# The second matrix product of seven token blocks as seven block products (Strassen's scheme, Winograd's form), with its operand sums on VectorE

## The chip, the core and the metric

One NeuronCore of a Trainium2 chip. TensorE (PE) multiplies matrices into PSUM, VectorE (DVE) and ScalarE (ACT) work elementwise between SBUF and PSUM, GpSimd (POOL) and SyncE (SP) here mostly issue transfers. The metric is the device time of one execution in microseconds; lower is better.

## What is computed

Linear attention with a cosine weight, then a feed-forward layer with a sigmoid GELU. q, k, v have 8 batches, 8 heads, 576 tokens and 64 features; the layer has d_model 512 and d_ff 2048.

```python
def phi(x, c, s):
    r = np.maximum(x, 0.0)
    return np.concatenate([r * c, r * s], axis=-1)     # c, s: cos, sin of pi/2 * pos / S
q_p, k_p = phi(q, cos_w, sin_w), phi(k, cos_w, sin_w)
kv  = np.einsum('bhsf,bhsd->bhfd', k_p, v)
z   = np.sum(k_p, axis=2)
num = np.einsum('bhsf,bhfd->bhsd', q_p, kv)
den = np.einsum('bhsf,bhf->bhs', q_p, z)[..., None] + 1e-06
x   = (num / den) as (B * S, 512)
h   = x @ w_in                                          # 512 -> 2048: the first product
g   = h * (1.0 / (1.0 + np.exp(-1.702 * h)))
out = g @ w_out                                         # 2048 -> 512: the second product
```

## The kernel before

The order of all work is written out by hand: each engine runs its instructions in the order in which the program names them, and semaphores hold an instruction until its operands are there and its target is free. A transfer belongs to the queue of the engine that issues it, so on SP and POOL a transfer that waits also holds those behind it.

**Blocks.** Of each batch 512 tokens form one block; the last 64 tokens of every batch, the tails, are gathered in `xt` and go through both products together at the end. Batch 0 is laid out in its own way and runs first (L474 to L614, together with the beginning of block 1 in `start_block`, L452). The loop at L643 then makes blocks 1 to 7. While block b is in its two products, everything for the attention of batch b + 1 is made beside it.

**One pass of the loop, in program order:**
- First product (`mm1`, L391): 16 chunks `fc` of 128 of the 2048 hidden features, each four matmuls of 512 columns (L383, the tokens are the columns) into a PSUM bank, then the GELU on ScalarE (`gelu`, L386), which writes the chunk as bf16, 128 features by 512 tokens, into a buffer `g` of its own. Block 1 has its first five chunks in `start_block`.
- Ahead of its first chunk: the weighted relu of q for batch b + 1 (`trig_q`, L189, ten instructions on VectorE), each of five chunks followed by a transposing transfer on SP into `qT` (`qturn_dma`, L223).
- Ahead of its second chunk: the same for k, and the copy of v to bf16 (`kv_operands`, L624), then `load_q` for batch b + 2 on SP.
- Between the products: `kv_next` (L616), the product of k and v for batch b + 1 into a buffer of `pat` (PSUM, two buffers), and its evacuation `kvs` by VectorE. In block 1 it stands behind the first token tile of the second product.
- Second product (`mm2`, L427): four tiles `t` of 128 tokens. A tile is 16 matmuls (L432): the weights loaded into the array are 128 features by 128 tokens of `g`, the columns that stream are 512 columns of `w_out_sb`. ScalarE evacuates a tile to `ysb` (L436), POOL sends it out (L439). Token 4p + t of a block is row p of tile t.
- Between half tiles: `x_next` (L637) for the five token tiles of batch b + 1. Each is a numerator on TensorE (`num_mm`, L328, into `pat`), three instructions on VectorE (`num_div`: L339, L341, L343, giving `xn`) and a transposing transfer on SP into `xT` (`xturn_dma`, L372). Behind `x_next(3)` stands `load_kv` (L146) for batch b + 2 on SP.
- In block 7 there is no next batch. The tails go through the first product (`mm1_tails`) and the second (tile 4 of `mm2`) ahead of its own second product, whose last tile is made as two halves of 256 columns so that the last transfer is short.

**Layouts of k and v.** Batches 1 and 2 have k and v in `kf`, `vf` with nine tokens a partition and two heads on the two halves of the partitions (`load`, L124; `trig`, L165; `vcopy`, L191; `kv_mm`, L236: 72 matmuls with 64 rows each). Batches 3 to 7 have four tokens a partition and all 128 partitions (`load_chunks`, L127; `trig_q` with `kr2`; `kv_chunks`, L244: 40 matmuls of 65 columns).

**Buffers.** `pmm` has four PSUM banks, used in turn by both products; `gpool` has 20 buffers `g` of 128 by 512; `ypool` four buffers `ysb`.

Of the kernel before, what the change touches and what calls it, by code (L numbers as in the profile page):

```python
# [14 lines left out]
MAX = mybir.AluOpType.max  # L15
PSUM = bass.MemoryType.PSUM
# [3 lines left out]
def kernel(  # L20
# [9 lines left out]
    nc = tc.nc  # L30
# [12 lines left out]
    gpool = ctx.enter_context(tc.tile_pool(name="gpool", bufs=20))  # L43
# [17 lines left out]
    kf, vf = [t[:, 0:NI * S].rearrange("p (i e) -> p i e", i=NI) for t in (kf2, vf2)]  # L61
    vb = raw("vb", BF16)
# [44 lines left out]
    kr = one.tile([128, NS, NI, 128], BF16, name="kr")  # L107
    vt = one.tile([128, NS, NI, VW], BF16, name="vt")
# [8 lines left out]
    nc.gpsimd.memset(vt[:, :, :, 64:66], 1.0)  # L117
# [5 lines left out]

    def load(t, src, b, eng=nc.gpsimd):  # L124
        eng.dma_start(out=t, in_=src_of(src, b))
# [20 lines left out]
    def load_kv(b):  # L146
        if b < 3:
            load(kf, k, b, nc.sync)
            load(vf, v, b, nc.sync)
        else:  # L150
            load_chunks(kf2, k, b, nc.sync)
            load_chunks(vf2, v, b, nc.sync)
# [38 lines left out]
    def vcopy(i0, i1, act=False):  # L191
        o = vt[:, :, i0:i1, 0:64].rearrange("p j i e -> p i j e")
        i = vf[:, i0:i1].rearrange("p i (j e) -> p i j e", e=64)
        if act:
            nc.scalar.activation(o, i, AF.Copy)
        else:
            nc.vector.tensor_copy(o, i)
# [188 lines left out]
    def gelu(fc):  # L386
        g = gpool.tile([128, MT], BF16, name="g")
        nc.scalar.activation(g, hp.pop(fc), AF.Gelu_apprx_sigmoid)  # L388
        gT[fc] = g
# [37 lines left out]
    def mm2(b, t, lo, hi, c0=0, c1=d_model, end=False):  # L427
        if lo == 0:
            yp[b, t, c0] = pmm.tile([128, d_model], F32, name="mm")
        for fc in range(lo, hi):  # L430
            w = gT[fc][:, ts(t, 128)] if t < 4 else gt[:, fc, ts(b // 2, 128)]
            nc.tensor.matmul(yp[b, t, c0][:, c0:c1], w, w_out_sb[:, fc, c0:c1],  # L432
                             start=(fc == 0), stop=(fc == FC - 1))
        if hi == FC:
            ysb = ypool.tile([128, d_model], F32, name="ysb")
            nc.scalar.activation(ysb[:, c0:c1], yp[b, t, c0][:, c0:c1], AF.Identity)  # L436
            for p0, n, dst in rows(b, t):
                eng = nc.sync if end else nc.gpsimd
                eng.dma_start(out=dst[:, c0:c1], in_=ysb[p0:p0 + n, c0:c1])  # L439

    def idle(n, cols=512):
        w = pmm.tile([128, 512], F32, name="mm")
        for _ in range(n):
            nc.tensor.matmul(w[:, 0:cols], warm[:, 0:128], warm[:, 0:cols], start=True, stop=True)
# [3 lines left out]

    def vt_rhs(r, i, j):
        return vt[r, j, i, 0:65]  # L450
# [48 lines left out]
    load(kf, k, 1)  # L499
# [72 lines left out]
    load(vf, v, 1)  # L572
# [4 lines left out]
    for j in range(NS):  # L577
        trig(kr, kf, j)
# [7 lines left out]
    vcopy(0, 2)  # L586
    vcopy(2, 4, act=True)
# [7 lines left out]
    kv_open()  # L595
    kv_mm(0, 4, vt_rhs, 0, 65)
    kv_evac(0, 4)
# [18 lines left out]
    def kv_next(b):  # L616
        if b < 3:
            kv_open()
            kv_mm(0, 4, vt_rhs, 0, 65)
            kv_evac(0, 4)  # L620
        else:
            kv_chunks()

    def kv_operands(b):  # L624
        if b < 3:
            for j in range(NS):
                trig(kr, kf, j)
            vcopy(0, 4)
        else:
            for c in range(5):  # L630
                trig_q(c, dst=kr2, src=kf2)
            for c0, c1, n in ((0, 4, 128), (4, 5, 64)):
                i = vf2[:, 0:2048] if c0 == 0 else vf2[0:64, 2048:2560]
                nc.vector.tensor_copy(vt2[0:n, c0:c1, :, 0:64],  # L634
                                      i.rearrange("p (h c d) -> p c h d", h=H, c=c1 - c0))
# [5 lines left out]


    for b in range(1, B):  # L643
        nb = b + 1 if b + 1 < B else None
        f0 = 5 if b == 1 else 0
        for fc in range(f0, FC):
# [4 lines left out]
            if nb is not None and fc == f0 + 1:  # L651
                kv_operands(nb)

                if nb + 1 < B:
                    load_q(nb + 1, nc.sync)
            mm1(b, fc)
        if nb is not None:
            x_open(nb)
        if nb is not None and b > 1:
            kv_next(nb)  # L660
        if nb is None:
            for fc in range(FC):
                mm1_tails(fc)
            for u in range(1, B, 2):
                mm2(u, 4, 0, FC, end=(u > 3))
        for t in range(4):
            if nb is None:
                for c in range(2 if t == 3 else 1):
                    n = 256 if t == 3 else 512
                    mm2(b, t, 0, FC, c * n, c * n + n, end=True)  # L670
                continue
            for u in range(2):
                mm2(b, t, 8 * u, 8 * u + 8)
                s = 2 * t + u
                if s == 1 and b == 1:

                    kv_next(nb)
                c = s if b > 1 else s - 1
                if b == 1 and s == 2:
                    x_next(nb, 0)  # L680
                if 0 <= c < 5 and (b > 1 or c > 0):
                    x_next(nb, c)
                if c == 3 and nb + 1 < B:
                    load_kv(nb + 1)
# [30 lines left out]
```

## Time and profile before

| what | value |
| --- | --- |
| runs | 291.19, 291.25, 291.77 us, median 291.25 |
| span of the profiled execution, first to last instruction | 289.4 us |
| granted TensorE clock | 1.000 |
| VectorE busy, block from 142.2 to 172.3 | 15.55 us, 38 instructions |
| ScalarE busy, same block | 11.94 us, 20 instructions |
| mean DMA share, same block | 0.87 |
| DMA share 172 to 180, 180 to 187, 187 to 195, 195 to 202 | 1.14, 0.94, 0.72, 0.67 |
| transposing transfers into qT: number, median from issue to landing | 35, 3.5 us |
| transposing transfers into xT: the same | 24, 2.7 us |
| k of batches 3 to 7, issue to landing | 6.9 us |
| v of batches 3 to 7, issue to landing | 11.0 us |

The page gives the profiled execution's span; a time of its own beside that is not among the runs. Times in the views are microseconds from the start of the span. The duration of a VectorE instruction overlaps the beginning of the next: the relus of 128x512 last 0.48 us and start 0.395 us apart. A line of the chain of waits in order of time has start, duration, engine, buffer, line and number of instructions; a line of the groups has the busy time, the mean of one in ns, and the idle time ahead of them with what ended most of it; a line of the timeline has start, duration, engine, line, operation, and in brackets how long the engine had been idle and what it waited for. The DMA share is the busy share of 16 engines summed over queues, so that it can come out over 1.

### The profile page before, as it was taken

What the parts mean: (1) busy time and instruction counts of PE and PEld (TensorE: products, weight loads), DVE (VectorE), ACT (ScalarE), POOL (GpSimd) and SP (SyncE); (2) the same over time, 40 slices, a digit from 0 to 9 for tenths busy, and PEclk for the clock granted to TensorE, in tenths of its full rate; (3) what the DMA queues carried; (4) which work ended last, traced back from release to release, by engine and by line L of the source; (5) the groups of instructions that cost most, each with busy time, mean ns of one, the idle gap of its engine ahead of it and who ended that gap; (6) DMA issues with size and microseconds to landing.
All of it is one profiled execution on the core that took longest, in us unless ns stands there. A gap on an engine that the chain in (4) does not pass through costs nothing.

```text
span 289.4 us, 5412 instructions
## 1 busy us (share of the span) xinstructions
PE 282.1 (97%) x2140; PEld 154.9 (54%) x2172; DVE 121.9 (42%) x323; ACT 128.0 (44%) x223; POOL 37.1 (13%) x69
## 2 busy tenths in 40 slices
PE   8999999999999999999999999999999999999995
PEld 2675646755555554555455545554555455554444
DVE  4834435772657266624670567148614300000000
ACT  6966644662146314631364126511760157761111
POOL 6683004100110011001100110001000100002000
PEclk9999999999999999999999999999999999999999
DMA  7999999999699899996999589967992610002322
GB/s 242 242 214 292 284 236 202 354 309 223 162 226 241 200 219 251 230 219 158 228 286 215 127 228 257 203 177 200 290 157 61 113 55 1 2 0 45 86 89 73
DMA packets 83545, 53.51 MB, mean 185 GB/s; under 512 B 57888, under 2 KB 78112, under 8 KB 83520
## 3 DMA queue, kind: packets, MB, share of 16 engines
q1 hardware_dynamic: 77456, 36.97, 57.2%
q0 software_dynamic: 6064, 16.19, 20.6%
q8 instruction: 17, 0.28, 0.4%
q14 instruction: 8, 0.07, 0.1%
HBM read 36.70 MB, written 9.44 MB: 159 GB/s over the span
## 4 chain that ended last, share of the span: by engine, by line
PE 92%; DMA 3%; ACT 2%; DVE 1%; issue 1%; ACTq 0%; POOL 0%
PE mm L432 42%; PE mm L383 37%; PE mm L411 4%; PE at L328 3%; DMA vb<-in_v_dram 2%; PE at L249 2%; PE at L241 1%; ACT g L388 1%; DMA kf<-in_k_dram 1%; PE at L360 1%; PE mm L404 1%; DVE xn L343 0%; PE mm L209 0%; ACT xT L367 0%; DVE xh L309 0%
## 5 line engine op out<-in xcount | busy, mean ns | idle before, releaser
L432 PE MATMUL mm<-w_out_sb,g 128*128 128x512 bf16 (+1 forms) x508 | 116.1, 372 | 1.2 <-issue 0.2
L383 PE MATMUL mm<-xT,w_in 128*128 128x512 bf16 (+1 forms) x582 | 112.1, 348 | 0.5
L388 ACT ACTIVATE g<-mm 128x512 bf16<-128x512 f32 x128 | 75.6, 598 | 32.5 <-PE mm L383 32.4
L383 PEld LDWEIGHTS <-w_in 128*128 128x128 bf16 x592 | 60.6, 113 | 48.7
L432 PEld LDWEIGHTS <-g 128*128 128x128 bf16 x528 | 48.8, 98 | 49.6
L436 ACT ACTIVATE ysb<-mm 128x512 f32<-128x512 f32 (+1 forms) x37 | 21.7, 586 | 111.2 <-PE mm L432 111.2
L439 POOL DMA_DIRECT2D out_dram<-ysb x36 | 19.7, 548 | 221.3 <-ACT ysb L436 221.3
L343 DVE TENSOR_TENSOR xn<-at,inv 128x512 bf16<-128x512 f32 x39 | 27.0, 691 | 1.3
L339 DVE TENSOR_SCALAR den<-at 128x8 f32<-128x8 f32 x36 | 6.0, 166 | 29.8 <-PE at L328 29.7
L328 PEld LDWEIGHTS <-qT 128*128 128x128 bf16 x312 | 14.4, 98 | 7.5
L189 DVE TENSOR_SCALAR qn<-qf,cosw 128x512 bf16<-128x512 f32 (+1 forms) x33 | 15.8, 478 | 3.9 <-DMA qf<-in_q_dram 3.9
L189 DVE TENSOR_SCALAR kr<-kf,cosw 128x512 bf16<-128x512 f32 (+1 forms) x25 | 12.0, 480 | 11.9 <-DMA kf<-in_k_dram 11.9
L328 PE MATMUL at<-kvs,qT 128*128 128x65 bf16 x312 | 15.8, 193 | 0.0
L189 DVE TENSOR_SCALAR qn<-qf,sinw 128x512 bf16<-128x512 f32 (+1 forms) x33 | 15.8, 478 | 0.0
L252 DVE CAST kvs<-at 128x520 bf16<-128x520 f32 x5 | 3.5, 702 | 27.3 <-PE at L249 27.3
L432 PE MATMUL mm<-w_out_sb,gt 128*128 128x512 bf16 x62 | 13.9, 379 | 0.1
L411 PE MATMUL mm<-xt,w_in 128*128 128x448 bf16 x64 | 12.3, 352 | 0.0
L173 DVE TENSOR_SCALAR kr<-kf,cosw 128x256 bf16<-128x256 f32 x24 | 9.0, 376 | 7.4 <-DMA kf<-in_k_dram 7.4
L189 DVE TENSOR_SCALAR kr<-kf,sinw 128x512 bf16<-128x512 f32 (+1 forms) x25 | 12.0, 479 | 0.0
L634 DVE CAST vt<-vf 128x2048 bf16<-128x2048 f32 (+1 forms) x10 | 7.9, 820 | 6.6 <-DMA vf<-in_v_dram 6.6
L432 PEld LDWEIGHTS <-gt 128*128 128x128 bf16 x64 | 6.3, 98 | 7.5
L413 ACT ACTIVATE gt<-mm 128x448 bf16<-128x448 f32 x16 | 8.7, 543 | 3.3 <-PE mm L411 3.2
(93 smaller groups left out, 129.3 us busy)
## 6 DMA issues: line engine op xcount, KB each, us to landing
qf<-in_q_dram SPq DMA_DIRECT2D x6, 1024.0 KB, 6.3
out_dram<-ysb POOLq DMA_DIRECT2D x24, 256.0 KB, 4.0
kf<-in_k_dram SPq DMA_DIRECT2D x5, 1024.0 KB, 6.9
vf<-in_v_dram SPq DMA_DIRECT2D x5, 1024.0 KB, 11.0
w_out_sb<-in_moe_w_out_dram POOLq DMA_DIRECT2D x4, 512.0 KB, 17.7
out_dram<-ysb POOLq DMA_DIRECT2D x12, 128.0 KB, 6.3
kf<-in_k_dram POOLq DMA_DIRECT2D x1, 1152.0 KB, 13.4
vf<-in_v_dram POOLq DMA_DIRECT2D x1, 1152.0 KB, 21.0
```

The source lines that it names most:

```text
L173: eng.tensor_scalar(o, i, 0.0, w[:, j:j + 1], op0=MAX, op1=MUL)
L189: nc.vector.tensor_scalar(o, i, 0.0, sc, op0=MAX, op1=MUL)
L328: nc.tensor.matmul(ps[:, h // 4, ds((h % 4) * 65, 65)], qT[:, h, ts(c, 128)], kvs_of(h), start=not eps_too, stop=(not eps_too or h % 4 == ...
L343: nc.vector.tensor_tensor(xn, pv[:, :, :, 0:64], inv.unsqueeze(3).to_broadcast([128, 2, 4, 64]), op=MUL)
L383: nc.tensor.matmul(hp[fc][:, t0:t1], wcol(kc, fc), x[b][:, kc, t0:t1], start=(kc == 0), stop=(kc == KC - 1))
L388: nc.scalar.activation(g, hp.pop(fc), AF.Gelu_apprx_sigmoid)
L411: nc.tensor.matmul(hps[:, 64:B * 64], wcol(kc, fc), xt[:, kc, 64:B * 64], start=(kc == 0), stop=(kc == KC - 1))
L413: nc.scalar.activation(gt[:, fc, 64:B * 64], hps[:, 64:B * 64], AF.Gelu_apprx_sigmoid)
L432: nc.tensor.matmul(yp[b, t, c0][:, c0:c1], w, w_out_sb[:, fc, c0:c1], start=(fc == 0), stop=(fc == FC - 1))
L436: nc.scalar.activation(ysb[:, c0:c1], yp[b, t, c0][:, c0:c1], AF.Identity)
L439: eng.dma_start(out=dst[:, c0:c1], in_=ysb[p0:p0 + n, c0:c1])
L634: nc.vector.tensor_copy(vt2[0:n, c0:c1, :, 0:64], i.rearrange("p (h c d) -> p c h d", h=H, c=c1 - c0))
```

## The change

**The second product of blocks 1 to 7.** The block's activations are split in two token halves i and two feature halves j (A_ij: 256 tokens by 1024 features), `w_out` in two feature halves and two column halves (W_jk: 1024 by 256). Eight block products would give the four output blocks; the changed kernel makes seven:

| product | into bank | activations | weights |
| --- | --- | --- | --- |
| p1 | x | A00 | W00 |
| p2 | w | A01 | W10 |
| p6 | x, added to p1 | s2 = s1 - A00 | t2 = W11 - t1 |
| p5 | y | s1 = A10 + A11 | t1 = W01 - W00 |
| p7 | x, added | s3 = A00 - A10 | t3 = W11 - W01 |
| p3 | y, added to p5 | s4 = A01 - s2 | W11 |
| p4 | x, added | A11 | nt4 = W10 - t2 |

The outputs are out00 = p1 + p2, out11 = (p1 + p6 + p7) + p5, out01 = (p1 + p6) + (p5 + p3), out10 = p1 + p6 + p7 + p4. A product is two tiles of 128 tokens with eight matmuls of 256 columns each, 112 matmuls in all. A bank holds both tiles (two times 256 columns). ScalarE keeps copies of x after p1 and after p6 and of y after p5 (`keep`, in buffers `kept_*`), VectorE adds a bank and a copy into `ysb` (`join`, after p2, p7 and p3), ScalarE evacuates x after p4. Each output leaves as one transfer with pieces of 256 columns.

**Sums on VectorE.** The weight sums t1, t2, t3, nt4 are made once (`w_sums`, four instructions of 128x2048 bf16), ahead of the loop, into `wsum`. The activation sums are made in each block in two halves of four chunks (`g_sums`, eight instructions of 128x1024 bf16) into `sums`: s3 and the first half of s1, s2, s4 at chunk 12 of the first product, the second half of s1 and s2 after `x_next(0)`, that of s4 after p1. `g` becomes a buffer of four chunks (five buffers), so that a sum is one instruction.

**Places of other work.** In blocks 2 to 6 the k-v product stands ahead of chunk 14 of the first product, and `x_next(0)` ahead of p1; `x_next(1)` to `(4)` follow p1, p2, p6, p5. In block 1 the k-v product follows p2, `x_next(0)` and `(1)` follow p6, the others p5, p7, p3.

**k and v of batches 1 and 2** use the layout of batches 3 to 7; `kr` and `vt` go, batch 0's `kr` lies in `wsum`, its `vb` in `sums`.

```diff
-    gpool = ctx.enter_context(tc.tile_pool(name="gpool", bufs=20))
+    gpool = ctx.enter_context(tc.tile_pool(name="gpool", bufs=5))
...
-    vb = raw("vb", BF16)
+    sums = one.tile([128, 4, d_ff], BF16, name="sums")
+    vb = sums.rearrange("p n e -> p (n e)")[:, 0:NI * S].rearrange("p (i e) -> p i e", i=NI)
...
+    wsum = one.tile([128, 4, d_ff], BF16, name="wsum")
+    kr = wsum.rearrange("p n e -> p (n e)")[:, 0:NS * NI * 128].rearrange(
+        "p (j i f) -> p j i f", j=NS, i=NI)
...
     def load_kv(b):
-        if b < 3:
-            load(kf, k, b, nc.sync)
-            load(vf, v, b, nc.sync)
-        else:
-            load_chunks(kf2, k, b, nc.sync)
-            load_chunks(vf2, v, b, nc.sync)
+        load_chunks(kf2, k, b, nc.sync)
+        load_chunks(vf2, v, b, nc.sync)
...
     def gelu(fc):
-        g = gpool.tile([128, MT], BF16, name="g")
-        nc.scalar.activation(g, hp.pop(fc), AF.Gelu_apprx_sigmoid)
-        gT[fc] = g
+        if fc % 4 == 0:
+            gT[fc // 4] = gpool.tile([128, 4, MT], BF16, name="g")
+        nc.scalar.activation(gT[fc // 4][:, fc % 4], hp.pop(fc), AF.Gelu_apprx_sigmoid)
...
+    def w_sums():
+        tt = nc.vector.tensor_tensor
+        tt(wt["t1"], wq[0, 1], wq[0, 0], op=SUB)
+        tt(wt["t2"], wq[1, 1], wt["t1"], op=SUB)
+        tt(wt["t3"], wq[1, 1], wq[0, 1], op=SUB)
+        tt(wt["nt4"], wq[1, 0], wt["t2"], op=SUB)
...
+    def g_sums(names, h):
+
+        tt = nc.vector.tensor_tensor
+        o = {n: sg[n][:, ts(h, 4)] for n in sg}
+        for n in names:
+            if n == "s1":
+                tt(o[n], a_blk(1, h), a_blk(1, h + 2), op=ADD)
+            elif n == "s2":
+                tt(o[n], o["s1"], a_blk(0, h), op=SUB)
+            elif n == "s3":
+                tt(o[n], a_blk(0, h), a_blk(1, h), op=SUB)
+            else:
+                tt(o[n], a_blk(0, h + 2), o["s2"], op=SUB)
...
+    def wino_mm(p, c):
+        name, to, a, w = PRODUCTS[p]
+        for fc in range(HF):
+            if isinstance(a, str):
+                lhs = sg[a][:, fc, ts(c, 128)]
+            else:
+                f = a[2] * HF + fc
+                lhs = gT[f // 4][:, f % 4, ds(a[1] * 256 + c * 128, 128)]
+            rhs = wt[w][:, fc] if isinstance(w, str) else wq[w][:, fc]
+
+            opens = name in OPENS and fc == 0 and (c == 0 or bank[to, "all"] is None)
+            nc.tensor.matmul(bank[to][c], lhs, rhs, start=opens,
+                             stop=(fc == HF - 1), skip_group_check=True)
...
+    def keep(n, src, act=True):
+        kept[n] = ypool.tile([128, 2, HD], F32, name=f"kept_{n}", bufs=1)
...
+            if act:
+                nc.scalar.activation(o, i, AF.Identity)
...
+    def join(b, i, n, src, with_, end):
+        y = ypool.tile([128, 2, HD], F32, name="ysb")
...
+            nc.vector.tensor_tensor(y, bank[src, "all"], kept[with_], op=ADD)
+        wino_out(b, i, n, 0, 2, y, end)
...
+    def wino_after(b, p, end=False):
+
+        name = PRODUCTS[p][0]
+        if name == "p1":
+            keep("p1", "x")
+        elif name == "p2":
+            join(b, 0, 0, "w", "p1", end)
+        elif name == "p6":
+            keep("u2", "x")
+        elif name == "p5":
+            keep("p5", "y")
+        elif name == "p7":
+            join(b, 1, 1, "x", "p5", end)
+        elif name == "p3":
+            join(b, 0, 1, "y", "u2", end)
...
+    w_sums()
 
     for b in range(1, B):
...
+            if fc == 12:
+                g_sums(("s3",), 0)
+                g_sums(("s3",), 1)
+                g_sums(("s1", "s2", "s4"), 0)
+            if fc == 14 and nb is not None and b > 1:
+                kv_chunks()
             mm1(b, fc)
         if nb is not None:
             x_open(nb)
-        if nb is not None and b > 1:
-            kv_next(nb)
...
+            if b > 1:
+                x_next(nb, 0)
+            g_sums(("s1", "s2"), 1)
+            at = {2 * p + 1: [p + 1] for p in range(4)} if b > 1 else {5: [0, 1], 7: [2], 9: [3], 11: [4]}
+            wino_open()
+            for p in range(7):
+                for c in range(2):
+                    wino_mm(p, c)
+                    s = 2 * p + c
+                    if c == 1:
+                        wino_after(b, p)
+                    if s == 3 and b == 1:
+                        kv_chunks()
+                    for c2 in at.get(s, ()):
+                        x_next(nb, c2)
+                        if c2 == 3 and nb + 1 < B:
+                            load_kv(nb + 1)
+                    if s == 1:
+                        g_sums(("s4",), 1)
+            continue
+        for fc in range(FC):
+            mm1_tails(fc)
+            if fc == 0:
+                g_sums(("s1", "s2", "s4"), 1)
+        for u in range(1, B, 2):
+            mm2(u, 4, 0, FC, end=(u > 3))
+        wino_open(last=True)
+        for p in range(7):
+            for c in range(2):
+                wino_mm(p, c)
+                if p == 6:
+                    wino_last(b, c)
+            wino_after(b, p, end=True)
```

## The prediction

> **What bounds the kernel.** I read the page's busy times first, then the chain that ended last, then one block of it in order of time (start, duration, engine, line).
>
> ```profile
> PE 282.1 (97%) x2140; PEld 154.9 (54%) x2172; DVE 121.9 (42%) x323; ACT 128.0 (44%) x223; POOL 37.1 (13%) x69
> ...
> PE 92%; DMA 3%; ACT 2%; DVE 1%; issue 1%; ACTq 0%; POOL 0%
> ```
>
> ```profile
> 182.53 3.61 PE mm L383 x16
> 186.15 1.21 PE at L249 x40
> ...
> 191.32 1.73 PE mm L432 x8
> 193.04 0.25 PE at L328 x8
> ```
>
> TensorE sets the end: from 13 us on it hardly stops. I call one pass of the loop at L643 a block. Blocks start (first L383 after the last L432) at 82.03, 112.13, 142.23, 172.34, 202.44: a steady block takes 30.1 us. It is 64 matmuls of L383, 64 of L432, one k-v product (1.21) and five numerators (0.25 each). Eight 512-column matmuls take 1.73, so one takes 0.216 and L432's 64 take 13.81: 13.81 x 2 + 1.21 + 1.25 = 30.1. Nothing else is on the path, so fewer TensorE columns shorten it as long as no operand comes late.
>
> **What seven products save.** A block's second product becomes 7 x 16 = 112 matmuls of 256 columns, each with its own weight load. The kernel has that form already, in the last token tile, where 16 of them lie between two evacuations (timeline, ScalarE):
>
> ```profile
> 284.47 0.38 ACT L436 ACTIVATE ysb<-mm 128x256 f32<-128x256 f32 x1 [1.15 <-PE mm L432]
> 286.21 0.38 ACT L436 ACTIVATE ysb<-mm 128x256 f32<-128x256 f32 x1 [1.36 <-PE mm L432]
> ```
>
> 1.74 / 16 = 0.109 us, half of 0.216 almost exactly. 112 x 0.109 = 12.20 against 13.81: 1.61 less per block, 11.3 in seven blocks (the last, 48 x 0.216 + 32 x 0.109 = 13.85 before, saves 1.65). [...]
>
> **What a sum costs.** No row has VectorE adding two SBUF tensors. The nearest (groups by shape; mean ns of one behind the bar):
>
> ```profile
> L343 DVE TENSOR_TENSOR xn<-at,inv 128x512 bf16<-128x512 f32 x39 | 27.0, 691 | 1.3
> L634 DVE CAST vt<-vf 128x2048 bf16<-128x2048 f32 x5 | 6.1, 1227 | 6.5 <-DMA vf<-in_v_dram 6.5
> L219 DVE COPY qT<-mm 128x1024 bf16<-128x1024 bf16 x2 | 1.3, 669 | 0.0
> ```
>
> The two-operand row does 512 elements in 691 ns, with the next instruction 0.61 later: one element per cycle, on f32 in PSUM. [...] A sum over 1024 all-bf16 elements so starts 0.61 after the last at two per cycle and 1.14 (0.61 + 0.53) at one. I take 0.61: its operands are the COPY's type (0.73 where it reads the sum before it: 0.69 and the 0.04 between L339 and L341). A weight sum over 2048 is 1.15, or 1.27 so linked; at one per cycle 2.2. [...]
>
> **Steady blocks (3 to 6).** VectorE is 15.5 of 30.1 us busy there (stretch 142.2 to 172.3) and gets 8 sums (5.3) and 3 joins (0.69 each, as L343): 22.9 of 28.5. In time from the block's start, v's copy ended at 9.05 (179.78 + 1.55 - 172.3), and a load's place before the block's end hardly changes: x_next(3) comes at 21.2 of 28.5, load_kv about 4.8 us before the end, 4.6 before. The query functions move from 4 us before the block's start to 1 before it, behind the last join; they then end at 2.9 and the key functions at 6.9, before v lands at 7.5. s3 ends at 10.3, the first s1, s2, s4 after gelu 11 (11.0) at 13.1; the kv evacuation (0.70) follows the product (12.07 + 1.21) at 14.0, and the first numerator wants it at 15.0. s1, s2 of the second half end at 17.7, p6 starts at 19.25. p7's join ends at 25.7, p4 overwrites that bank from 26.75. So the added VectorE work is hidden by 1 to 2 us everywhere: -1.61 x 4 = -6.4. Three of a block's four outputs now leave while k, v arrive, before it was two: 256 KB at some 270 GB/s (windows) is up to 0.95 us later for v; the evacuation has 1.0 us spare, and 0.95 more where the sums now wait for gelu.
>
> **Block 1.** Here the cover is missing. w_sums stands on VectorE ahead of the query functions (L189), and all is queued behind it:
>
> ```profile
> 53.38 0.69 DVE L343 TENSOR_TENSOR xn<-at,inv 128x512 bf16<-128x512 f32 x1
> 54.26 0.49 DVE L189 TENSOR_SCALAR qn<-qf,cosw 128x512 bf16<-128x512 f32 x1 [0.20 <-DMA qf<-in_q_dram]
> ```
>
> 54.0 + w_sums 4.7 (1.27 + 3 x 1.15) + 10 query functions at 0.395 (3.95) + 10 of keys (3.95, kf landed at 60.4) + v copy 1.5 = 68.1; two s3 to 69.3, s1, s2, s4 to 71.4, s1, s2 of the second half end at 72.8. TensorE: p1, p2 from 65.55 to 69.05, kv 1.21, to 70.25; p6 would end at 72.0, but 12 of its 16 matmuls need the last s2, so 74.15: **2.15 late**. Behind s2 on VectorE wait s4 (0.73), the p2 join (0.61) and the kv evacuation, which ends at 74.8; numerator 0 waits another **0.7**. Then p5, p7, p3, p4 with numerators end at 83.1. xn(3) comes behind p7's join (79.8), at 80.95; its transpose lands 2.4 to 2.7 later (xT's DMA row), 83.5, and block 2's first product waits **0.5**. Block 2 starts at 83.6, not 82.03: +1.6, though 1.6 was saved. Query transposes on SP start 4.7 later and end near 71, before numerator 0.
>
> **Block 2.** load_kv(3) follows the xT(3) transpose on SP: 82.15 in place of 79.04, 3.1 later while the block is 1.6 later.
>
> ```profile
> 79.04 0.58 SPq L128 DMA_DIRECT2D kf<-in_k_dram  x1
> ```
>
> ```profile
> 92.48 1.55 DVE L634 CAST vt<-vf 128x2048 bf16<-128x2048 f32 x2 [1.04 <-DMA vf<-in_v_dram]
> ```
>
> v's copy ends at 92.48 + 1.5 + 3.1 = 97.1; the product, now ahead of the last two chunks of the first layer, wants it at 83.6 + 12.1 = 95.7: 1.4 late. Five sums stand between copy and evacuation (to 100.35, evacuated 101.05): numerator 0 at 101.1 against 100.05, 1.05 late. 28.5 + 2.45 = 30.95: +0.85, and up to 0.95 more for the third output; I take 0.4.
>
> **The rest.** Block 7 has the tails' 26 us between sums and use: -1.65. Batches 1 and 2 need 40 matmuls (1.21) for 72 (1.19): nothing. k and v of batch 1 cost POOL two issues more (0.72 each by L130); behind them w_out's last quarter was issued at 24.0 and is needed at 45.2, v landed at 41.1 and is needed by 42.8. This 1.7 us hides it; at worst +1.0. The rewritten evacuations are four a block on ScalarE, as before.
>
> Sum: 1.6 + 1.25 - 6.4 - 1.65 = **-5.2 us**. The span goes from 289.4 to 284.2. The median of the runs, 291.25, is 1.85 over that span, which I carry over: **286.0**.
>
> **Rivals.**
> - *A, the sum above*: 284.5 to 288, chance 0.55.
> - *B, k3 and v3 come in time*: block 2 loses nothing, 2.85 less, so 283.2; with block 1 whole as well, 280 (291.25 - 11.3). For it: v needed 13.4 us from the issue of k to its copy here, but 12.1 in a steady block (167.64 to 179.78). Against: the DMA engines' share is 1.10 to 1.23 from 82 to 104, and nothing empties that stretch. 0.14.
> - *C, transfers late in every block*: mean share 0.87 over 30.1 us becomes 0.92 over 28.5, output pieces halve to 1 KB, and if v lands 3 us later the evacuation is 1 us late in blocks 3 to 6: 290. 0.13.
> - *D, the slower side: sums at one element per cycle*, as the two-operand row has it. w_sums 9.0; block 1's last s2 at 80.8, p6 10.15 late, numerator 0 1.25, x 0.35: +10.0. Block 2: 1.5 and 3.7 late, +3.6. Steady blocks 0.75 late: -0.85 x 4. Block 7 -1.65. Total +8.6: 300. Between 0.61 (-5.2) and 1.14 (+8.6) it decides at about 0.81 us per sum. For it: that row; against: the COPY row. 0.08. [...]
> - *E, a weight load for every 256 columns sets the pitch*: loads (98 ns, L432) not hidden, 112 x 0.207 = 23.2, +9.4 per block, some 357. The 0.109 above excludes nearly all of it: 0.01. [...]
> - *F, no change*: half of the steady gain lost to causes not seen, such as POOL's issues or w_out late, 289 to 293. 0.09.
>
> **Numbers.** The likeliest is A, 286.0. From 282.5 to 291 lie A, C, most of B and half of F, some 0.84. About 0.2% (0.6 us) can be told from no change. Faster: A, B, C and a third of F, less a slip, 0.83; within 0.2%: 0.04; slower: D, E and the rest of F, 0.13.
>
> **What would show it.** L432's place taken by 256-column matmuls with a pitch of 0.109 (E wrong); sums of 0.69 and 1.23 us (D wrong, if 1.2 and 2.3 right); blocks 3 to 6 of 28.5 us without a TensorE wait (C wrong); in block 1 TensorE waiting some 2 us in p6 on the s2 sum, in block 2 on the v copy at the k-v product, then on the kv evacuation (B wrong). A block 1 without a wait, or steady blocks over 29.5, would make the prediction wrong.

## The result, and the profile after

The changed kernel takes 287.9 us (median of 286.98, 287.65, 288.16, 289.41) beside 291.3 for the kernel before on the same chip: ratio 0.9887, 95% interval 0.9857 to 0.9917. It is faster, by 3.4 us and not by the 5.2 of the forecast. Its profiled execution took 286.98 with a span of 285.3. Medians and ranges below are of all executions of a kernel; the ratios leave out those more than 1.5% above that kernel's fastest.

The page's busy times and the engines' shares of the chain that ended last:

```profile
PE 272.3 (95%) x2403; PEld 186.6 (65%) x2428; DVE 175.9 (62%) x391; ACT 128.3 (45%) x225; POOL 43.7 (15%) x70
...
PE 81%; DMA 10%; DVE 6%; issue 1%; SPq 1%; ACT 0%; DVEq 0%
```

TensorE is 9.8 us less busy than before, but the span is only 4.1 shorter: VectorE and transfers, 4% of the chain before, are 16% of it now. Where they came in is read from the chain in order of time (start, duration, engine, line); the lines of L381 are the first matmuls of blocks 3 to 7:

```profile
57.17 11.24 DMA vf<-in_v_dram
68.50 1.55 DVE vt L195 x2
70.06 1.20 DVE sums L470 x2
...
75.97 0.62 DVE kvs L250
...
85.47 10.97 DMA vf<-in_v_dram
96.46 1.55 DVE vt L195 x2
...
101.27 0.62 DVE kvs L250
...
110.35 5.24 PE mm L503 x48
115.59 0.22 PE mm L381
...
144.12 0.22 PE mm L381
...
172.63 0.22 PE mm L381
...
201.16 0.22 PE mm L381
...
229.67 0.21 PE mm L381
```

Two things are to be seen. From 115.59 on the path is TensorE, up to the last evacuation: blocks 3 to 6 take 28.53, 28.51, 28.53 and 28.51 us, and 48 matmuls of 256 columns take 5.24, so 0.109 each. Ahead of that, between 57 and 77 us, the path runs through the load of v, VectorE's copy of it, the sums and the k-v evacuation: block 1. It does so once more from 85 to 102 us, with v of batch 3: block 2. The waits of both, from TensorE's timeline (the bracket is the idle time and what ended it):

```profile
69.78 1.57 PE L247 MATMUL at<-vt,kr 128*128 128x65 bf16 x40 [0.58 <-DVE vt L195]
72.64 0.61 PE L503 MATMUL mm<-wsum,sums 128*128 128x256 bf16 x4 [1.29 <-DVE sums L468]
74.70 1.48 PE L503 MATMUL mm<-wsum,sums 128*128 128x256 bf16 x12 [1.44 <-DVE sums L468]
76.63 0.67 PE L326 MATMUL at<-kvs,qT 128*128 128x65 bf16 x16 [0.45 <-DVE kvs L250]
85.54 12.28 PE L381 MATMUL mm<-xT,w_in 128*128 128x512 bf16 x54 [0.49 <-DMA xT<-xn]
101.94 0.41 PE L326 MATMUL at<-kvs,qT 128*128 128x65 bf16 x8 [0.90 <-DVE kvs L250]
```

The first five are 4.25 us before block 2 begins, at 85.54; the sixth is the only wait inside block 2. VectorE's timeline shows what a sum costs, and that VectorE itself stood waiting for k and v of batch 2:

```profile
54.00 1.22 DVE L451 TENSOR_TENSOR wsum<-w_out_sb 128x2048 bf16<-128x2048 bf16 x1
...
63.97 0.49 DVE L184 TENSOR_SCALAR kr<-kf,cosw 128x512 bf16<-128x512 f32 x1 [1.24 <-DMA kf<-in_k_dram]
...
68.50 1.55 DVE L195 CAST vt<-vf 128x2048 bf16<-128x2048 f32 x2 [0.49 <-DMA vf<-in_v_dram]
...
73.95 0.69 DVE L468 TENSOR_TENSOR sums<-sums,g 128x1024 bf16<-128x1024 bf16 x1
```

Those 1.24 + 0.49 us are not in the forecast. The last s2, for which p6 waits, ends at 74.64, not at 72.8.

### The profile page after: what moved, and what is told of

The parts are those of the page before. It is cut to its first block, busy times and chain, and to the rows that moved or that the text cites. A ratio compares the mean times of both kernels' runs of the same rounds, so it can differ in the third digit from the quotient of the medians.

```text
span 285.3 us, 5954 instructions
## 1 busy us (share of the span) xinstructions
PE 272.3 (95%) x2403; PEld 186.6 (65%) x2428; DVE 175.9 (62%) x391; ACT 128.3 (45%) x225; POOL 43.7 (15%) x70
## 4 chain that ended last, share of the span: by engine, by line
PE 81%; DMA 10%; DVE 6%; issue 1%; SPq 1%; ACT 0%; DVEq 0%
PE mm L381 31%; PE mm L503 28%; PE mm L430 10%; DMA vf<-in_v_dram 8%; PE mm L409 4%; PE at L326 3%; PE at L247 2%; DMA kf<-in_k_dram 2%; DVE vt L195 1%; PE at L358 1%; DVE sums L470 1%; DVE wsum L168 1%; PE mm L207 1%; PE mm L402 1%; DVE sums L468 1%
## 5 line engine op out<-in xcount | busy, mean ns | idle before, releaser
L381 PE MATMUL mm<-xT,w_in 128*128 128x512 bf16 (+1 forms) x571 | 112.4, 348 | 1.6 <-DMA xT<-xn 0.5
L381 PEld LDWEIGHTS <-w_in 128*128 128x128 bf16 x592 | 60.2, 113 | 47.2 <-DMA xT<-xn 0.8
L503 PEld LDWEIGHTS <-sums 128*128 128x128 bf16 x448 | 42.4, 98 | 7.8 <-DVE sums L468 3.1
L503 PE MATMUL mm<-wsum,sums 128*128 128x256 bf16 x336 | 39.9, 272 | 2.7 <-DVE sums L468 2.7
L503 PEld LDWEIGHTS <-g 128*128 128x128 bf16 x336 | 32.1, 98 | 4.0
L528 DVE TENSOR_TENSOR ysb<-mm,kept_p 128x512 f32<-128x512 f32 x13 | 8.9, 688 | 30.5 <-PE mm L503 30.5
L503 PE MATMUL mm<-w_out_sb,g 128*128 128x256 bf16 x224 | 26.4, 272 | 0.1
L184 DVE TENSOR_SCALAR kr<-kf,cosw 128x512 bf16<-128x512 f32 (+1 forms) x35 | 16.7, 476 | 6.7 <-DMA kf<-in_k_dram 6.7
L518 ACT ACTIVATE kept_p<-mm 128x512 f32<-128x512 f32 (+1 forms) x15 | 8.5, 570 | 20.9 <-PE mm L503 20.9
L184 DVE TENSOR_SCALAR kr<-kf,sinw 128x512 bf16<-128x512 f32 (+1 forms) x35 | 17.7, 505 | 0.0
L337 DVE TENSOR_SCALAR den<-at 128x8 f32<-128x8 f32 x36 | 5.8, 162 | 14.9 <-PE at L326 14.8
L430 PE MATMUL mm<-w_out_sb,g 128*128 128x512 bf16 x62 | 14.7, 379 | 0.1
L195 DVE CAST vt<-vf 64x512 bf16<-64x512 f32 (+1 forms) x13 | 9.7, 788 | 7.3 <-DMA vf<-in_v_dram 7.3
```

Of the source, the lines that this page charges most:

```text
L184: nc.vector.tensor_scalar(o, i, 0.0, sc, op0=MAX, op1=MUL)
L381: nc.tensor.matmul(hp[fc][:, t0:t1], wcol(kc, fc), x[b][:, kc, t0:t1], start=(kc == 0), stop=(kc == KC - 1))
L503: nc.tensor.matmul(bank[to][c], lhs, rhs, start=opens, stop=(fc == HF - 1), skip_group_check=True)
L518: nc.scalar.activation(o, i, AF.Identity)
L528: nc.vector.tensor_tensor(y, bank[src, "all"], kept[with_], op=ADD)
```

## The experiments

The theory after the result: the products and the sums cost what was forecast, block 1's chain on VectorE is as forecast too, and the loss is the layout of k and v of batches 1 and 2, priced at nothing. Rivals: block 1's chain is longer than forecast by itself; steady blocks lose; the finer transfers cost nothing. Each kernel was run beside the kernel before on the same chip; the median of that one lay between 291.2 and 291.34 in every group.

**The changed kernel again**, for its spread.

> The changed kernel once more, for the runs beside it and for its spread. Theory (time saved on TensorE, part of it lost in block 1 where the weight sums hold up VectorE's chain): 287 to 289 us, TensorE waits of 4.2 us in block 1 and 0.9 in block 2. Rival for the spread of its four runs (286.98 to 289.41, granted clock 0.988 to 0.999): the clock is granted lower in some executions because TensorE stands idle for stretches in block 1; then runs differ by up to 2.4 us with the clock, where the kernel before has 0.6.

287.29 (ten runs, 286.22 to 290.22), ratio 0.9877 (0.9845 to 0.991). In its trace p6's twelve matmuls, 1.48 above, took 2.74. Stretches of its trace (length, busy times of PE, PEld, DVE, ACT, POOL, then granted clock, DMA share, GB/s):

```profile
72.00:74.00 2.00, 0.61 (x4) 0.31 (x4) 1.93 (x4) 0.00 (x0) 0.00 (x0) 0.98 0.78 113
74.00:76.00 2.00, 1.65 (x8) 1.19 (x9) 1.97 (x4) 0.00 (x0) 0.08 (x1) 0.50 0.84 248
76.00:78.00 2.00, 2.00 (x26) 1.68 (x24) 0.62 (x4) 0.60 (x1) 0.67 (x1) 0.67 1.13 333
```

The same stretches of the changed kernel's first profile:

```profile
72.00:74.00 2.00, 0.61 (x4) 0.31 (x4) 1.93 (x4) 0.00 (x0) 0.00 (x0) 1.00 0.88 136
74.00:76.00 2.00, 1.30 (x12) 1.19 (x13) 1.97 (x4) 0.00 (x0) 0.00 (x0) 1.00 0.80 211
```

In the repeated run the granted clock is half for some 3.3 us right behind block 1's waits (all of 74 to 76, two thirds of 76 to 78); in the first profile, with waits of 1.29 and 1.44 us there against 0.87 and 1.45, it stays at 1.00. The mean clocks of all runs lie near 0.999, 0.994 and 0.988, and 1.7 us lost at half rate is 0.6% of the span: that fits none, one or two such stretches in a run. So the waits can cost more than their own length. The clock is not the whole of the spread, though: seven of the ten runs had 0.993 or 0.994, and they took from 287.01 to 290.22 us.

**The layout alone**, in the kernel before.

```diff
     def load_kv(b):
-        if b < 3:
-            load(kf, k, b, nc.sync)
-            load(vf, v, b, nc.sync)
-        else:
-            load_chunks(kf2, k, b, nc.sync)
-            load_chunks(vf2, v, b, nc.sync)
+        load_chunks(kf2, k, b, nc.sync)
+        load_chunks(vf2, v, b, nc.sync)
...
-    load(kf, k, 1)
+    load_chunks(kf2, k, 1, nc.gpsimd)
...
-    load(vf, v, 1)
+    load_chunks(vf2, v, 1, nc.gpsimd)
```

> The kernel before with the second part of the change alone: k and v of batches 1 and 2 four tokens a partition. The prediction had this at nothing: 291.3 +- 0.5. Rival: the loads of batches 1 and 2 become slower or later, q's transposes and the loads on SP with them, and the v copy of batch 2 ends behind the k-v product's place in block 1 (69.2 us): about +1 us, 292.3, with a TensorE wait at the k-v product of block 1.

298.09 (294.6 to 299.16), ratio 1.019 (1.0125 to 1.0255): slower by 3.3 to 7.3 us in three of the four executions, by 7.9 in the last. Its profiled execution is the 294.6 one. TensorE now waits in the loop's lead-in (0.29 for a query transpose at the numerator of 53.8) and, most of all, at the start of block 2:

```profile
85.00 5.34 PE L380 MATMUL mm<-xT,w_in 128*128 128x512 bf16 x24 [1.75 <-DMA xT<-xn]
```

So the term is not nothing, and the next runs ask what it is in the changed kernel, and of which batch.

**Batch 1 alone back in the old layout**, in the changed kernel. Buffers of its own for the old layout of both batches do not fit into SBUF beside the sums (the last pool wants 10.9 kB a partition, 1.1 are left), so batch 1's `kr` lies in `wsum` and its `vt` in `sums`, which are written later, and batch 2 stays as it is.

```diff
-    load_chunks(kf2, k, 1, nc.gpsimd)
+    load(kf, k, 1)
...
-    load_chunks(vf2, v, 1, nc.gpsimd)
+    load(vf, v, 1)
...
-    for c in range(5):
-        trig_q(c, dst=kr2, src=kf2)
+    for j in range(NS):
+        trig(kr, kf, j)
```

> The changed kernel with k and v of batch 1 alone back in the old layout (nine tokens a partition; its kr and vt lie in wsum and sums, which are written later). Theory: the new layout's loads hold up GpSimd's queue (v of batch 1 issued at 23.9 and 27.6 in place of 20.05, w_out's last quarter at 28.5 in place of 24.0), and everything of batch 1 and the loads behind it come 2 us late; with the old layout v is issued near 20, q of batch 2 on SP near 47.4 in place of 49.4 to 50.2, k of batch 2 is no longer waited for, block 1's waits fall from 4.2 to some 2.5 us: 285.5 beside 287.3 for the changed kernel. Rival (the layout does not matter inside the changed kernel, the sums alone make block 1 late): 287.3 +- 0.5.

285.24 (284.81 to 286.54), ratio 0.9803 (0.9774 to 0.9832): 2.05 less than the changed kernel (1.7 between the spans of the two profiled executions, 283.6 and 285.3). TensorE's timeline:

```profile
70.71 0.61 PE L523 MATMUL mm<-wsum,sums 128*128 128x256 bf16 x4 [0.30 <-DVE sums L488]
72.76 1.48 PE L523 MATMUL mm<-wsum,sums 128*128 128x256 bf16 x12 [1.45 <-DVE sums L488]
74.69 0.67 PE L346 MATMUL at<-kvs,qT 128*128 128x65 bf16 x16 [0.45 <-DVE kvs L265]
...
83.91 12.28 PE L401 MATMUL mm<-xT,w_in 128*128 128x512 bf16 x54 [0.80 <-DMA xT<-xn]
```

The last s2 ends at 72.71 (forecast 72.8) and block 2 starts at 83.91 (forecast 83.6): with batch 1's layout gone, block 1 is what the prediction worked out, and VectorE waits for no load. The rival that the chain itself is longer is excluded. How the layout gets there is read from the queues. GpSimd's timeline of the changed kernel:

```profile
23.92 0.90 POOL L127 DMA_DIRECT2D vf<-in_v_dram  x1 [2.98 <-DMA w_in<-in_moe_w_in_dram]
27.58 0.90 POOL L129 DMA_DIRECT2D vf<-in_v_dram  x1 [2.76 <-DMA kf<-in_k_dram]
28.47 0.74 POOL L150 DMA_DIRECT2D w_out_sb<-in_moe_w_out_dram  x1
```

The same of the kernel before:

```profile
20.05 0.78 POOL L125 DMA_DIRECT2D vf<-in_v_dram  x1
24.04 0.55 POOL L155 DMA_DIRECT2D w_out_sb<-in_moe_w_out_dram  x1 [3.22 <-DMA w_in<-in_moe_w_in_dram]
```

With four transfers of k and v in place of two, GpSimd stands twice until an earlier transfer has landed, and w_out's last quarter leaves at 28.5 instead of 24.0. SP's queue is later too: batch 1's five query transposes last 12.32 us from 36.93 (10.25 from 36.26 in this run), and the load of q for batch 2 leaves at 49.43 instead of 46.69. Behind it SP stands longer in the second piece of k for batch 2; the changed kernel, then this run:

```profile
52.17 4.82 SPq L129 DMA_DIRECT2D kf<-in_k_dram  x1
```

```profile
49.47 2.46 SPq L136 DMA_DIRECT2D kf<-in_k_dram  x1
```

So v of batch 2 leaves at 57.17 instead of 52.04. This k and this v are what VectorE waited 1.73 us for. That undoing batch 1's layout ends these waits is shown; how GpSimd's queue makes SP's transposes and issues longer is read from the order alone.

**The small pieces on SP**: the 64-partition parts of batch 1's k and v issued by SP, the rest by GpSimd.

```diff
-    def load_chunks(t, src, b, eng):
+    def load_chunks(t, src, b, eng, eng2=None):
...
-        eng.dma_start(out=t[0:64, 2048:2560].rearrange("p (h e) -> p h e", h=H),
+        (eng2 or eng).dma_start(out=t[0:64, 2048:2560].rearrange("p (h e) -> p h e", h=H),
...
-    load_chunks(kf2, k, 1, nc.gpsimd)
+    load_chunks(kf2, k, 1, nc.gpsimd, nc.sync)
...
-    load_chunks(vf2, v, 1, nc.gpsimd)
+    load_chunks(vf2, v, 1, nc.gpsimd, nc.sync)
```

> The changed kernel with the second piece of k and of v of batch 1 (64 partitions, 512 pieces of 256 bytes each) issued by SP in place of GpSimd. If it is the number of pieces in GpSimd's queue that makes v and w_out's last quarter wait: v is issued near 20 to 24 and w_out's last quarter near 24 to 25 in place of 28.5, and about half or more of the 2.05 us between the changed kernel and the one with batch 1 in the old layout comes back: 286.2 or less beside 287.3. If the smaller pieces themselves are slow on the DMA engines: 287.3, with SP's q transposes of batch 1 still taking 12.3 us or more.

287.39 (286.8 to 287.84), ratio 0.9877 (0.986 to 0.9893): no better than the changed kernel. GpSimd's hold-up is gone in good part (v leaves at 20.19, w_out's last quarter at 25.16), the query transposes of batch 1 take 10.46, the load of q for batch 2 leaves at 48.09, and block 2 starts at 84.89: 0.65 of the 1.63 us between 85.54 and 83.91 come back. The rest shows in two places: the weight sums start at 54.53 (53.99 with batch 1 old), and VectorE still waits 0.57 for k of batch 2, in whose second piece SP again stands 4.99 us. GpSimd's queue is thus part of the cause and not all of it; what makes SP stand there (the finer pieces on the DMA engines would be one reading) was not separated.

**Block 1 by eight products**, with the weight sums behind it, both batches in the new layout.

```diff
-    w_sums()
...
-            if fc == 12:
+            if fc == 12 and b > 1:
...
+            if b == 1:
+                for t in range(4):
+                    for u in range(2):
+                        mm2(b, t, 8 * u, 8 * u + 8)
...
+                w_sums()
+                continue
```

> The changed kernel with block 1 by eight products as before (no sums in it), the weight sums on VectorE behind block 1's numerators. Theory: block 1 gives back the 1.6 us of six products' saving but has none of the 4.2 us of waits, and block 2 gets k and v earlier (0.9): about 3 to 3.5 us less than the changed kernel, 284.6. Rival: the 4.7 us of weight sums now delay block 2's queries and keys, and the wait only moves there: no gain, or 1 us.

287.63 (285.04 to 289.7), ratio 0.9841 (0.9784 to 0.9899): 2 to 3 us over what was expected (the profiled execution took 286.62), and no gain on the changed kernel that is clear of the spread (the intervals of the two ratios overlap). Block 1's waits for sums are gone, and another stands in their place, at block 2's first product:

```profile
86.56 3.62 PE L381 MATMUL mm<-xT,w_in 128*128 128x512 bf16 x16 [3.03 <-issue]
```

The view names no releaser, but the first product's operand is `xT`, and its transposes, issued from 75.07 to 81.56, landed 4.3 to 6.4 us after their issue, against 2.4 to 2.6 in the changed kernel. There the load of q for batch 3 had left SP 5.5 us ahead of the first of them (72.70, 78.24), here 2.6 (72.49, 75.07). The reading is that block 1's own lateness had kept the two apart; the runs of batch 2 below bear on it.

**The same with batches 1 and 2 in the old layout** (the edits of two runs above together, that with batch 1 in the old layout and that with eight products in block 1, and `if b < 3` back in `load_kv` and in the relu and copy of k and v).

> Block 1 by eight products, weight sums behind it, and k, v of batches 1 and 2 in the old layout, so that seven products run in blocks 2 to 7 only and nothing of the kernel before is changed up to block 1's end. Theory: block 1 ends at 82.0 as before; blocks 2 to 7 save 1.61 each, 9.7, less 1.0 in block 2 for the k-v evacuation behind five sums: 282.6, with the runs within 0.6 us of each other, because no stretch without TensorE work is left and no load is late. Rival (the spread and part of the loss come with the sums or the 256-column matmuls): 285 to 288 and a spread of 2 us or more.

283.18 (282.52 to 283.5), ratio 0.9722 (0.9707 to 0.9736): 8.0 us faster than the kernel before and 4.1 faster than the changed one; no other kernel here is faster clear of the noise, and the mean clock is 1.000 in all four. Two waits are left, 0.51 for xT at block 2's start and 0.60 for the k-v evacuation in block 2.

**Batch 2 alone in the new layout**: in the run just told, and in the kernel before (here the second, where `kv_next` and `kv_operands` have the same edit).

```diff
-        if b < 3:
+        if b < 2:
             load(kf, k, b, nc.sync)
             load(vf, v, b, nc.sync)
```

> The changed kernel with block 1 by eight products, weight sums behind it, batch 1 in the old layout and batch 2 alone in the new one. It stands between the run with both batches old (283.18 us) and the run with both new (287.63). Theory: the cost of the layout is what batch 1's four transfers on GpSimd do ahead of w_out's last quarter and of the q transposes in block 0, so batch 2, loaded by SP in the middle of block 0, costs nothing: 283.2, within 0.4. Rival: batch 2's smaller pieces take DMA time in block 0 as well: 284.5 or more. The clock should stay at 1.000 in either case, since block 1 has no short waits.

> The kernel before with batch 2 alone in the new layout (both batches new: 298.1 us, and 294.6 in its profiled run). Theory as above: 291.2, no change, and no wait of TensorE that the kernel before does not have. Rival, batch 2's pieces count: 293 or more, with the q transposes of block 0 or xT of block 1 late.

The first gave 283.3, ratio 0.9756 (0.9715 to 0.9797): four runs from 282.95 to 283.42, and two of 285.88 and 287.05. The second gave 294.28, ratio 1.005 (1.0017 to 1.0082): four runs from 291.27 to 291.92, and six from 293.36 to 296.81. Neither theory holds as it was put: batch 2's layout costs nothing in some runs and 2 us or more in others. The second's trace (295.52) is of a late one, the first's (283.42) of one that is not; block 2's first product in the second, then in the first:

```profile
85.95 13.98 PE L383 MATMUL mm<-xT,w_in 128*128 128x512 bf16 x63 [3.44 <-DMA xT<-xn]
```

```profile
82.51 12.25 PE L401 MATMUL mm<-xT,w_in 128*128 128x512 bf16 x55 [0.42 <-DMA xT<-xn]
```

The second's SP timeline:

```profile
55.65 4.12 SPq L130 DMA_DIRECT2D vf<-in_v_dram  x1
59.89 10.75 SPq L223 DMA_TRANSPOSE qT<-qn  x5
70.69 0.59 SPq L128 DMA_DIRECT2D qf<-in_q_dram  x1
...
74.05 6.64 SPq L372 DMA_TRANSPOSE xT<-xn  x4
```

SP stands until 59.77 in the issue of v's pieces, so the query transposes start at 59.89, not at 55.21 as before, and the load of q behind them at 70.69, not at 67.33. That leaves 3.4 us, not 6.3, between this load of 1152 KB and the first xT transpose, and xT landed 4.7 to 7.3 us after issue (2.4 to 3.7 before). In the first's trace, though, SP's order is the same: query transposes from 59.92, the load of q at 70.73, xT 2.9 us behind it. There xT landed 4.2 to 6.8 us after issue, and TensorE waited 0.42 for it.

Nine traces show the issue and the landing: the kernel before, the changed kernel twice, and the runs of the layout alone, of batch 1 old, of eight products in block 1 (both batches new, both old, batch 2 new) and of batch 2 alone. In them block 2's xT landed 4.1 to 7.3 us after issue where 3.4 us or less lay between the load of q for batch 3 and the first xT transpose (four traces), and 2.4 to 4.4 where 5.4 or more did (five). TensorE then waited 0.42, 1.75, 3.03 and 3.44 us in the four, and 0 to 0.80 in the five. So late landing goes with the order on SP; why it costs a run much or little stays open.

**The k-v evacuation of block 2 ahead of the sums**, in the kernel with eight products in block 1 and both batches old (283.18 us).

```diff
-            if fc == 12 and b > 1:
+            if fc == 12 and b > 2:
                 g_sums(("s3",), 0)
                 g_sums(("s3",), 1)
                 g_sums(("s1", "s2", "s4"), 0)
             if fc == 14 and nb is not None and b > 1:
                 kv_chunks()
+            if fc == 14 and b == 2:
+                g_sums(("s1", "s2"), 0)
+            if fc == 15 and b == 2:
+                g_sums(("s3",), 0)
+                g_sums(("s3",), 1)
+                g_sums(("s4",), 0)
```

> As the run before (old layout, eight products in block 1), and in block 2 the k-v evacuation stands ahead of the sums on VectorE. Theory: the last wait of block 2 goes, 0.9 us less than that run: 281.7. Rival (the sums are then late for p6): equal or slower.

282.9 (282.56 to 283.28), ratio 0.9715 (0.9701 to 0.973): the same. Block 3 started 1.36 us earlier (110.53 in place of 111.89; 0.68 of it was there at block 2's start, where xT was not waited for in this execution), and then waited:

```profile
126.93 0.42 PE L350 MATMUL at<-kvs,qT 128*128 128x65 bf16 x8 [0.90 <-DVE kvs L269]
```

The wait moved one block on, and the gain went with it: block 4 starts at 140.59, and at 140.57 without the edit. The chain ahead of this wait runs through the load of v (12.63 us from 108.80) and VectorE's copy of it; VectorE waited for that load 2.85 us here and 1.31 without the edit, where the chain in block 3 is TensorE's own.

**How much slack the steady blocks have**: the s3 sums of blocks 3 to 6 made twice (1.2 us more on VectorE ahead of the evacuation), in the changed kernel.

```diff
                 g_sums(("s3",), 0)
                 g_sums(("s3",), 1)
+                if 2 < b < 7:
+                    g_sums(("s3",), 0)
+                    g_sums(("s3",), 1)
```

> The changed kernel with the two s3 sums of blocks 3 to 6 computed twice, 1.2 us more on VectorE ahead of the k-v evacuation. The prediction gave that evacuation 1.0 us to spare, and 0.95 more where the sums wait for gelu 11; the changed kernel's trace shows s1 waiting for nothing in block 3 and the evacuation ending 0.6 us ahead of the numerator. Theory: blocks 3 to 6 take 28.5 to 29.1 us, a TensorE wait on kvs of 0 to 0.6 in each. Rival (VectorE is hidden by much more): 28.5 and no wait.

289.34 in one run (span 287.6; the clock fell to 0.50 from 76 to 78, in block 1, here too, so the total says little). The waits say more: 0.39 in block 3, none in blocks 4 and 5, 0.58 in block 6, all at the first numerator for the evacuation. With 1.2 us added, the slack in this execution is thus 0.6 to 0.8 us in blocks 6 and 3 and at least 1.2 in blocks 4 and 5.

**The weight sums made twice**, in the kernel with batch 1 in the old layout.

```diff
     w_sums()
+    w_sums()
```

> The changed kernel with batch 1 in the old layout (285.24 us) and the four weight sums computed twice. Theory (they stand on the path of block 1, ahead of p6): 4.6 us more on VectorE is 4.6 us more wait of TensorE in block 1, now in part at the k-v product; 289.9, and up to 1.7 more in runs whose granted clock falls to half for one stretch, as it did from 74 to 77.4 us in the run of the changed kernel here. Rival (VectorE has slack in block 1): 285 to 286.

290.7 (289.3 to 291.34), ratio 0.9972 (0.9956 to 0.9988). 4.66 us more on VectorE moved block 2's start by 4.77, from 83.91 to 88.68, and p6's second wait ended 4.72 later (77.48 for 72.76): the weight sums lie on the path in full. The median rose by 5.5, and the mean clock fell to 0.980 to 0.994.

**Two of the weight sums on GpSimd**, in the same kernel.

```diff
     def w_sums():
         tt = nc.vector.tensor_tensor
...
+        tt = nc.gpsimd.tensor_tensor
         tt(wt["t3"], wq[1, 1], wq[0, 1], op=SUB)
         tt(wt["nt4"], wq[1, 0], wt["t2"], op=SUB)
```

> The changed kernel with batch 1 in the old layout, and t3 and nt4 computed on GpSimd, which is idle from 52 to 73 us; t1, t2 stay on VectorE. Theory: 2.3 us less on VectorE ahead of p6, whose waits of 1.75 in that kernel go; t3 and nt4 are needed only by p7 and p4 (76 and 80 us); by GpSimd's relu row (4.6 ns per element) they take 9.4 us each and end near 71: 283.3. Rival: GpSimd and VectorE hold each other up, VectorE's relus of block 1 take longer than 0.48 us, or t3, nt4 end later than 76 and 80 us: 285 or more.

290.04 (289.53 to 290.77), ratio 0.9964 (0.995 to 0.9978): 4.8 us worse than all four on VectorE. GpSimd's timeline:

```profile
52.26 4.08 POOL L474 TENSOR_TENSOR wsum<-w_out_sb 128x2048 bf16<-128x2048 bf16 x1
58.76 4.24 POOL L475 TENSOR_TENSOR wsum<-w_out_sb,wsum 128x2048 bf16<-128x2048 bf16 x1 [2.42 <-DVE wsum L472]
```

and VectorE's of the same time:

```profile
53.97 3.44 DVE L471 TENSOR_TENSOR wsum<-w_out_sb 128x2048 bf16<-128x2048 bf16 x1
57.45 1.23 DVE L472 TENSOR_TENSOR wsum<-w_out_sb,wsum 128x2048 bf16<-128x2048 bf16 x1
58.59 0.48 DVE L191 TENSOR_SCALAR qn<-qf,cosw 128x512 bf16<-128x512 f32 x1
58.99 4.29 DVE L191 TENSOR_SCALAR qn<-qf,sinw 128x512 bf16<-128x512 f32 x1
```

A sum of 1.22 lasted 3.44 and ended 1.07 after GpSimd's, and a relu of 0.48 lasted 4.29 and ended 0.28 after the second: VectorE stood until GpSimd was done, each time. That is 2.2 + 3.8 us more on VectorE for 2.3 less, and its last s2 ends 3.75 later (76.46 for 72.71). Behind that the clock fell in this trace (mean 0.982): the k-v product's 40 matmuls took 2.50 from 71.60 and p5's sixteen 2.76 from 79.95, against 1.37 and 1.91 with all four on VectorE, and block 2 starts 6.34 later, at 90.25.

## Why the prediction was right, and where it was off

**Products.** 0.109 us per 256-column matmul and 28.5 us per steady block, both as forecast: no steady block waits, so rivals E and C are out, and so is F's loss of half the steady gain.

**Sums.** 0.69 us for 1024 and 1.22 for 2048, where the prediction had 0.69 and 1.23, and rival D 1.2 and 2.3: rival D is out. The prediction's one and two per cycle are a ratio, read from 512 elements in 691 ns and 1024 in 669; no view gives the cycle itself. In time, the sums cost 0.52 ns an element (0.53 us for the 1024 between 0.69 and 1.22), the two-operand rows on f32 in PSUM 1.04 (691 ns for 512 and 424 for 256, L343 and L309 before). The prediction chose by the type, which the sums share with the COPY row; that the type makes the difference is not shown: the cast of v reads f32 from SBUF and costs 0.52 too (1227 ns for 2048, 694 for 1024).

**Block 1.** The forecast chain held to 0.1 us at the last s2 and 0.3 at block 2's start, once batch 1's layout was undone. The waits were placed rightly; in that run p6's 2.15 was 0.30 + 1.45, the numerator's 0.7 was 0.45, xT's 0.5 was 0.80. In the changed kernel itself the layout made p6's 1.29 + 1.44 and added 0.58 at the k-v product.

**The step that was mis-sized** is the layout of k and v: "nothing", "at worst +1.0". It measured 2.05 us for batch 1 in the changed kernel (1.63 of it at block 2's start in the profiled executions), and 3.3 to 7.3 for both batches in the kernel before. The cover that the prediction named, 1.7 us for v and w_out of block 0, was the wrong one: in the profiled execution neither was late. What came late stood further back on another queue, SP's: k and v of batch 2. The prediction counted GpSimd's two issues more and stopped there.

**Block 2** lost less than forecast: 30.05 us, not 28.5 + 2.45 + 0.4. v's copy was taken to end 14.9 us after the issue of k, as before; it ended 13.85 after (84.16 to 98.01), and the k-v product, forecast 1.4 late, followed its chunks without a wait. The evacuation was 0.90 late, for 1.05, and the 0.4 for a third output did not show. So rival B held for the product and not for the evacuation. The block is 1.53 longer than a steady one; the 0.90 is all of that which a bracket names.

**Slack.** 1 to 2 us was forecast for the steady blocks; 0.6 to 0.8 is there in two of them, and at least 1.2 in the other two.

**The sum.** In spans: forecast 284.2, profiled 285.3. Block 2 started 1.94 later (85.54 for 83.6) and was 1.30 shorter (30.05 for 31.35); blocks 3 to 6 took 114.08 for 114.0; from block 7's start to the end it was 55.63, 1.23 less than before (289.4 - 232.54 = 56.86) where 1.65 was forecast, as the end came 3.2 us after the last evacuation in place of 2.8. 1.94 - 1.30 + 0.08 + 0.42 = 1.14. The other 0.8 between 286.0 and the median of 287.9 is how far that median lies over the profiled execution (0.92), less 0.17 for the smaller step from span to time. A halved clock can be part of it (mean 0.994 and 0.988 in the runs of 287.65 and 289.41), but the run of 288.16 had 0.998; what made it late is not known. The forecast had no term for this. Its range, 284.5 to 288, just holds the result, and that is in part luck: the layout was put too low, and block 2's loss 1.30 too high.

**Seven products in block 1** do not pay: with batch 1 old and batch 2 new, seven give 285.24 and eight 283.3 by the median, though two of the eight's six runs (285.88, 287.05) are no better. In the profiled executions, both at a clock of 1.000, block 2 starts at 83.91 and 82.51. The forecast held this too: it had the block's end at 83.6 with seven and 82.03 with eight. With both batches in the new layout the two kernels could not be told apart.

## What to carry to other kernels

Price a change of layout by its issues on every queue and by what stands behind each of them, not by the wait of the data that it moves: here the data itself was in time, and the next batch's was not. A block that must first make operands for a cheaper product can lose more than the product saves; here it was better to make the one-time sums where the engine has time and to start one block later. When a wait is removed, look for the next one at the same engine: twice here (xT behind block 1, the evacuation behind block 2) it took the gain or most of it.

## What the hardware showed unexpectedly

**Waits behind which the clock can halve.** In the repeated run of the changed kernel TensorE was busy 0.61 us of 72 to 74 and 1.65 of 74 to 76, no single wait was over 1.5 us, and the granted clock was half for 3.3 us. The first profile's waits there, 1.29 and 1.44 us against 0.87 and 1.45, left the clock at 1.00. Behind other waits three more traces have a lower clock. With the s3 sums made twice it was 0.71, 0.50 and 0.94 in the stretches of 2 us from 74 to 80, 1.7 us lost, which is 3.4 at half rate; with the weight sums made twice the mean of 0.994 over 287.5 us comes to the same. With GpSimd's sums the mean was 0.982 over 288.7, 5.2 us lost, some 10 at half rate if no other was granted. The kernel with eight products in block 1 and both batches old, without these waits, had 1.000 in every run and a spread of 1.0 us, where the changed one had 4.0. That the waits bring the halving rests on these comparisons; what decides whether it comes, and how long it lasts, was not found.

**VectorE held up beside a GpSimd sum.** The two GpSimd sums over 2048 took 4.08 and 4.24 us. The VectorE instructions beside them, a two-operand sum and a one-operand relu, lasted 3.44 and 4.29 us in place of 1.22 and 0.48, and ended 1.07 and 0.28 us after the GpSimd sum. By what the one holds the other no view shows.
